# A seven-product first layer for the last two units of an attention and MLP kernel, and a new order for its head and tail

## The chip, the cores and the metric

The kernel runs on one core of one Trainium2 chip. The metric is device time in microseconds (us), the median of several runs. A profiled execution gives the span from the first to the last instruction, and its own time beside it.

## The reference

Inputs are q, k and v, each 4 batches × 8 heads × 768 positions × 64, eight memory positions per head (`mem_k`, `mem_v`), a gain `g_ln` of 512, and the weights `w_ch1` (512 × 2048) and `w_ch2` (2048 × 512), all float32. The two parts, shortened:

```python
for c in range(768 // 32):                         # chunks of 32 queries
    l_start, r_end = max(0, 32*c - 16), min(768, 32*c + 32 + 8)
    k_full = concatenate([mem_k, k[:, :, l_start:r_end]], axis=2)
    v_full = concatenate([mem_v, v[:, :, l_start:r_end]], axis=2)
    a = softmax(q[:, :, 32*c : 32*c + 32] @ k_full.T / sqrt(64))
    out[:, :, 32*c : 32*c + 32] = a @ v_full
x  = out.transpose(0, 2, 1, 3).reshape(4, 768, 512)
xn = (x - mean(x)) / sqrt(var(x) + 1e-6) * g_ln
y  = x + maximum(xn @ w_ch1, 0) @ w_ch2
```

## The kernel before

The 3072 tokens are 24 tiles `t` of 128 tokens, six per batch. Two tiles are a unit `u`, so there are 12 units (`NP = 12`). Operands are float16, sums float32.

Attention for a tile: `qk_products` (scores, L320), `row_max` and `less_max` on VectorE (L329, L332), `weights` (exponential, ScalarE, L342), `pt_products` and `pt_copy` (transpose of the weights, L351, L359), `val_products` (L371, into the two-bank buffer `two`), `tokens` (division by the row sum, VectorE, L380 to L387). Then the norm: `shift` subtracts the mean (GpSimd L394 or ScalarE L398), `square` and `root_of` give the scale, `x_products` transposes the tile (L427) and `x_copy` multiplies by the gain into `xT` (VectorE, L436).

The MLP for a unit of 256 tokens: the first layer is `up_products` (L455): eight groups `s`, each two blocks of 128 hidden columns times four slices of 128 inputs, so eight products of 256 columns. `relu_up` moves a group to `rT` (L447). The second layer is `down7` (L532): the unit's two tiles and the halves of the hidden and the output dimension make a 2 × 2 block product, done with seven block products of eight matmuls in place of eight. For this it needs four sums of `rT` blocks (`r_sum` into `RS`, VectorE, L526) and, once per kernel, four sums of weight blocks (`w2_sum` into `T`, L511). `add_to` adds each product, scaled, to the token tile `xs` (L539), and `store` writes the tile out (L544, SyncE's queue).

PSUM has eight banks: `one` (2), `upb` (2), `dnb` (2) and `two` (2 together). A product waits until the last reader of its bank is done.

The schedule is manual: each engine runs its instructions in the order in which the program names them. Three parts follow one another:

- A head, L603 to L977, written out item by item: loads, transposes, attention of the first ten tiles, units 0 and 1, and the first layer of unit 2. It contains `warm` products (L599): multiplications of zeros that nobody reads, 21 in all. Loads go out on GpSimd's queue; eight can be under way, and a ninth waits for the first.
- A loop over units 3 to 11 with 16 steps each. Even steps do `up` of unit `u` (banks `upb`), odd steps `down7` of unit `u − 1` (banks `dnb`); a table `plan` puts the attention, norm and `r_sum` work of later tiles at given steps.
- A tail: `down7` of unit 11, with its sums.

Of the kernel before, what the change touches and what calls it, by code (L numbers as in the profile page):

```python
# [11 lines left out]
ALU = mybir.AluOpType  # L12
AX = mybir.AxisListType


@with_exitstack
def kernel(
# [416 lines left out]
    def x_copy(t, pv):  # L434
        i = t % 2
        nc.vector.tensor_tensor(  # L436
            out=xT[(t // 2) % 3][:, :, 128 * i : 128 * i + 128],
            in0=pv.rearrange("p (d c) -> p d c", d=4),
            in1=free(g_col, 0, [[1, 4], [0, 128]]), op=ALU.mult,
        )  # L440
# [53 lines left out]

    def w2_block(i, o, n):
        c = w2c[2 * i + n]
        return c[:, :, 256 * o : 256 * o + 256]
# [15 lines left out]
    def r_block(u, i, o):  # L513
        return rT[u % 2][:, 8 * o : 8 * o + 8, 128 * i : 128 * i + 128]

    def r_sum(u, k, lo=0, hi=8):

        if k == 0:
            a, b, op = r_block(u, 1, 0), r_block(u, 1, 1), ALU.add
        elif k == 1:  # L520
            a, b, op = RS[0], r_block(u, 0, 0), ALU.subtract
        elif k == 2:
            a, b, op = r_block(u, 0, 0), r_block(u, 1, 0), ALU.subtract
        else:
            a, b, op = r_block(u, 0, 1), RS[1], ALU.subtract
        nc.vector.tensor_tensor(  # L526
            out=RS[k][:, lo:hi, :], in0=a[:, lo:hi, :], in1=b[:, lo:hi, :], op=op
        )
# [19 lines left out]
    def down7_products(u, part, p):  # L548
# [4 lines left out]
        def total(k):  # L553
            return lambda n: T[k][:, n, :]

        left, right, add = (
            lambda: (r_block(u, 0, 0), block(0, 0), False),
            lambda: (r_block(u, 0, 1), block(1, 0), False),
            lambda: (RS[1], total(1), True),
            lambda: (RS[0], total(0), False),  # L560
            lambda: (RS[2], total(2), True),
            lambda: (RS[3], block(1, 1), True),
# [22 lines left out]
    def ready_v(i, eng):  # L585
        eng.memset(V[i][:, :, :, 64:VW], 1.0)
        eng.memset(V[i][0:16, 0, :, :], 0.0)
        eng.memset(V[i][96:128, NG - 1, :, :], 0.0)
        eng.tensor_copy(
            out=V[i][96:128, NG - 1, :, 64:VW],  # L590
            in_=free(last[96:128, 0:1], 0, [[0, H], [0, VW - 64]]),
        )

# [14 lines left out]
    nc.vector.memset(V[0][:, 0:4, :, 64:VW], 1.0)  # L608
    nc.vector.memset(V[0][0:16, 0, :, 64:VW], 0.0)
# [4 lines left out]
    warm(7, upb[0])  # L614
    load_octets(0, 0, k, 0, 0, 48, (0,))
    load_octets(0, 0, k, 0, 0, 48, (1,))
    load_octets(1, 0, q, 0, 0, 32, (1,))
    copy_on("A")(out=mem16, in_=mem32)
    make_identity(nc, identity)
    mem_products(one[0])  # L620
    mem_copy(one[0], "V")
    mem_cols(KT[0], memT[:, 0:4, :], "V")
    mem_ends(KT[0], memT[:, 0:4, :], "A")
    load_octets(1, 0, q, 0, 0, 32, (0,))
    warm(6, one[1])
    tk0 = turn(raw[0][0], 0, 48, one[1])
    load_octets(2, 0, v, 0, 0, 48, (0,))
    mem_cols(VT, memT[:, 16:20, :], "V")
    load_octets(2, 0, v, 0, 0, 48, (1,))
    to_stream(KT[0], tk0, 0, "V", 48, 0)  # L630
    load_octets(1, 1, q, 0, 32, 64, (0,))
    tk1 = turn(raw[0][0], 1, 48, upb[0])
    to_stream(KT[0], tk1, 1, "V", 48, 0)
    load_octets(1, 1, q, 0, 32, 64, (1,))
    load_octets(0, 1, k, 0, 48, 48, (1,))
    warm(1, upb[1])
    tq1 = turn(raw[1][0], 1, 32, upb[1])
    to_rows(0, tq1, 1, "V", 32, 0, 0, 16)
    mix_into(whole[0], raw[2][0], 0, 96, "V")
    load_octets(2, 1, v, 0, 48, 48, (0,))  # L640
    load_octets(2, 1, v, 0, 48, 48, (1,))
    tq0 = turn(raw[1][0], 0, 32, dnb[0])
    load_octets(0, 1, k, 0, 48, 48, (0,))
    to_rows(0, tq0, 0, "A", 32, 0, 0, 16)
    warm(4, dnb[1])
    s0 = qk_products(0, dnb[1])
    tv0 = turn_whole(whole[0], 0, 96, one[0])
    to_stream(VT, tv0, 0, "V", 48, 0)
    load_w1(0)
    mix_into(whole[0], raw[2][0], 1, 96, "A")  # L650
    to_rows(0, tq0, 0, "A", 32, 0, 16, 32)
    nc.gpsimd.memset(V[0][:, 4:NG, :, 64:VW], 1.0)
    to_rows(0, tq1, 1, "A", 32, 0, 16, 32)
    tv1 = turn_whole(whole[0], 1, 96, one[1])
    to_stream(VT, tv1, 1, "A", 48, 0)
    s1 = qk_products(1, upb[0])
    row_max(1, s1)
    warm(2, dnb[0])
    v2 = v_products(2, dnb[0])
    load_octets(1, 0, q, 1, 0, 48, (0,))  # L660
    load_v_group(1, 11, 1)
    load_w1(3)
    v1 = v_products(1, upb[1])
    load_w1(1)
    mix_into(whole[3], raw[1][1], 1, 128, "A")
    v0 = v_products(0, one[0])
    v_copy(0, v0, "A")
    row_max(0, s0)
    v_copy(1, v1, "A")
    less_max(0, s0)  # L670
    weights(0)
    load_octets(1, 0, q, 1, 0, 48, (1,))
    less_max(1, s1)
    weights(1)
    tQ1 = turn_whole(whole[3], 1, 128, one[1])
    nc.gpsimd.memset(last, 1.0)
    mix_into(whole[3], raw[1][1], 0, 128, "V")
    v3 = v_products(3, one[0])
    v_copy(2, v2, "V")
    p0 = pt_products(0, dnb[1])  # L680
    pt_copy(0, p0, "V")
    mix_into(whole[2], raw[2][1], 1, 96, "V")
    v_copy(3, v3, "A")
    mix_into(whole[2], raw[2][1], 0, 96, "P")
# [4 lines left out]
    p1 = pt_products(1, upb[1])  # L689
    pt_copy(1, p1, "V")  # L690
    val_products(0)
    tokens(0)
    tV1 = turn_whole(whole[2], 1, 96, upb[0])
    load_w2(0)
    to_rows(0, tQ1, 1, "A", 64, 32)
    tQ0 = turn_whole(whole[3], 0, 128, dnb[0])
    mix_into(whole[1], raw[0][1], 0, 96, "A")
    tV0 = turn_whole(whole[2], 0, 96, dnb[1])
    to_stream(VT, tV0, 0, "A", 48, 48)
    load_w1(2)  # L700
# [36 lines left out]
    up_products(0, 1, upb[1])
    relu_up(0, 1, upb[1], "A")
    row_max(2, s2)
    less_max(2, s2)  # L740
    weights(2)
    up_products(0, 0, upb[0])
    up_products(0, 2, one[0])
    relu_up(0, 2, one[0], "A")
    up_products(0, 6, dnb[0])
    p2 = pt_products(2, dnb[1])
    load_v_group(1, 9, 0)
    v_copy(10, v10, "A")
    load_v_group(1, 9, 1)
    root_of(1)  # L750
    pt_copy(2, p2, "V")
    nc.gpsimd.memset(V[0][96:128, NG - 1, :, :], 0.0)
    nc.gpsimd.tensor_copy(
# [3 lines left out]
    load_v_group(1, 6, 1)  # L757
    up_products(0, 7, upb[1])
    relu_up(0, 6, dnb[0], "A")
    relu_up(0, 7, upb[1], "A")  # L760
    val_products(2)
    v9 = v_products(9, one[0])
    relu_up(0, 0, upb[0], "V")
    tokens(2)
    shift(2, "A")
    square(2)
    ready_v(1, nc.gpsimd)
    s3 = qk_products(3, one[1])
    row_max(3, s3)
    less_max(3, s3)  # L770
    up_products(0, 3, dnb[1])
    v_copy(9, v9, "V")
    down_products(0, 0, dnb[0])
    weights(3)
    down_products(1, 0, upb[0])
    relu_up(0, 3, dnb[1], "A")
    x2 = x_products(2, upb[1])
    x_copy(2, x2)
    up_products(0, 5, one[1])
    relu_up(0, 5, one[1], "V")  # L780
    p3 = pt_products(3, one[0])
    root_of(2)
    load_v_group(1, 4, 1)
    pt_copy(3, p3, "V")
    lq01 = turn_whole(mixed[1], 1, 96, dnb[1])
    to_rows(1, lq01, 1, "A", 48, 0)
    up_products(0, 4, upb[1])
    relu_up(0, 4, upb[1], "A")
    load_octets(1, 1, q, 1, 48, 48, (0,))
    val_products(3)  # L790
    tokens(3)
    v8 = v_products(8, one[1])
    s4 = qk_products(4, one[0])
    down_products(1, 1, upb[0])
    row_max(4, s4)
    less_max(4, s4)
    down_products(0, 1, dnb[0])
    v_copy(8, v8, "A")
    lq00 = turn_whole(mixed[1], 0, 96, dnb[1])
    shift(3, "A")  # L800
    nc.gpsimd.memset(memv16[:, :, :, 64:VW], 1.0)
    x3 = x_products(3, upb[1])
    x_copy(3, x3)
    down_products(0, 2, dnb[0])
    w2_sum(0)
    load_v_group(1, 0, 0)
    weights(4)
    square(3)
    load_octets(1, 1, q, 1, 48, 48, (1,))
    p4 = pt_products(4, one[1])  # L810
    load_octets(0, 1, k, 1, 48, 48, (1,))
    pt_copy(4, p4, "A")
# [272 lines left out]
```

## Time and profile before

| | |
|---|---|
| median of 3 runs | 225.61 us (224.96 to 226.55) |
| the profiled execution | 225.04 us, span 223.3 us |
| TensorE busy | 215.1 us, 96% of the span |
| VectorE, ScalarE, GpSimd busy | 164.8 us, 130.3 us, 114.4 us |
| granted TensorE clock | 1.0 in every slice |
| moved by DMA | 23.24 MB, mean 104 GB/s |

A row of a timeline has the start, the duration, the engine, the source line and the operation, then output and inputs, how many were merged, and the idle time before them with what ended it. Durations of successive instructions on an engine overlap by about a tenth of a microsecond, and TensorE's products overlap more, so their cost is read from start to start. A row of a group has busy time, the mean in ns of one, and the idle time before with its releasers.

### The profile page before, as it was taken

The numbers are of one execution on the slowest core, as the hardware profiler recorded it, in microseconds if no ns is written. First come the engines' busy times: TensorE is split into PE (matmuls) and PEld (weight loads), VectorE is DVE, ScalarE is ACT, GpSimd is POOL, SyncE is SP. The second block draws the span as 40 slices with busy tenths as digits, with TensorE's granted clock in tenths as the row PEclk, the third lists the DMA queues.
The fourth block names the chain that finished last, engine by engine and source line by source line (L and its number), as shares of the span: only waits on it lengthen the run. The fifth ranks groups of instructions, "written<-read, shape, count | busy, mean of one in ns | idle before, by whom it ended". The sixth has DMA issues, their size and how long they took to land.

```text
span 223.3 us, 8291 instructions
## 1 busy us (share of the span) xinstructions
PE 215.1 (96%) x3597; PEld 188.9 (85%) x3597; DVE 164.8 (74%) x367; ACT 130.3 (58%) x248; POOL 114.4 (51%) x195
## 2 busy tenths in 40 slices
PE   6987999999999999999999999999999999999994
PEld 2555877689888899999999999999999899999983
DVE  1588667979898886994886996994875876747373
ACT  3198875877785288288357198198266365443320
POOL 7958399989889717957346927321121130320000
PEclk9999999999999999999999999999999999999999
DMA  5999999999999994995934975942002002011022
GB/s 74 191 204 204 211 212 208 134 175 113 126 98 135 164 113 80 121 92 96 185 29 108 132 91 110 91 76 97 3 3 94 3 3 94 3 50 47 0 97 97
DMA packets 43449, 23.24 MB, mean 104 GB/s; under 512 B 30004, under 2 KB 39796, under 8 KB 43364
## 3 DMA queue, kind: packets, MB, share of 16 engines
q0 software_dynamic: 38416, 14.48, 55.3%
q1 hardware_dynamic: 4996, 8.22, 12.8%
q8 instruction: 28, 0.46, 0.8%
q14 instruction: 9, 0.07, 0.1%
HBM read 29.02 MB, written 6.29 MB: 158 GB/s over the span
## 4 chain that ended last, share of the span: by engine, by line
PE 78%; DMA 14%; POOL 3%; DVE 1%; issue 1%; ACT 0%; SPq 0%; POOLq 0%
PE upb L455 30%; PE dnb L532 28%; DMA w1c<-in_moe_w_ch_dram 5%; PE two L371 3%; DMA raw<-in_q_dram 3%; DMA V<-memv 3%; PE one L272 3%; DMA raw<-in_k_dram 2%; PE one L320 2%; PE one L427 2%; POOL raw L105 2%; PE one L351 2%; PE dnb L455 2%; PE upb L481 2%; PE dnb L481 2%; PE one L455 1%
## 5 line engine op out<-in xcount | busy, mean ns | idle before, releaser
L455 PE MATMUL upb<-xT,w1c 128*128 128x256 f16 x656 | 84.7, 273 | 0.3 <-ACT rT L447 0.3
L455 PEld LDWEIGHTS <-w1c 128*128 128x128 f16 x768 | 81.1, 114 | 2.3 <-issue 0.5
L447 ACT ACTIVATE rT<-upb 128x512 f16<-128x512 f32 x81 | 47.1, 597 | 30.9 <-PE upb L455 30.8
L539 DVE SCALAR_TENSOR_TENSOR xs<-dnb,rstd,xs 128x256 f32<-128x256 f32 x75 | 36.1, 481 | 24.1 <-PE dnb L532 23.1
L532 PEld LDWEIGHTS <-RS 128*128 128x128 f16 x352 | 33.6, 98 | 3.6 <-issue 0.2
L342 ACT ACTIVATE P<-sub 128x512 f16<-128x512 f32 x24 | 15.1, 631 | 31.4 <-DVE sub L332 31.3
L532 PE MATMUL dnb<-T,RS 128*128 128x256 f16 x256 | 32.8, 273 | 0.0
L394 POOL TENSOR_SCALAR xn<-xs,nmean 128x512 f16<-128x512 f32 x18 | 12.7, 704 | 31.2 <-PE upb L455 17.5
L532 PEld LDWEIGHTS <-rT 128*128 128x128 f16 x264 | 25.3, 98 | 2.5
L414 POOL TENSOR_SCALAR veps<-ssq 128x1 f32<-128x1 f32 x24 | 4.8, 200 | 40.7 <-ACT sq L407 40.0
L532 PE MATMUL dnb<-w2c,rT 128*128 128x256 f16 x176 | 22.6, 273 | 0.0
L526 DVE TENSOR_TENSOR RS<-rT 128x1024 f16<-128x1024 f16 (+2 forms) x23 | 15.3, 664 | 8.9 <-ACT rT L447 8.9
L407 ACT ACTIVATE sq<-xs,nmean 128x512 f16<-128x512 f32 x24 | 17.3, 722 | 0.1
L381 DVE CUSTOM_DVE_ANT_1 xs<-two,rec 128x512 f32<-128x512 f32 x24 | 16.6, 692 | 0.8
L418 POOL TENSOR_TENSOR rstd<-veps,mhalf 128x1 f32<-128x1 f32 x24 | 14.2, 591 | 2.0
L436 DVE TENSOR_TENSOR xT<-one,g_col 128x512 f16<-128x512 f16 x18 | 12.3, 686 | 3.5 <-PE one L427 3.3
L114 POOL DMA_DIRECT2D V<-in_v_dram x16 | 13.4, 838 | 0.8 <-PE dnb L532 0.7
L359 ACT COPY PT<-one 128x512 f16<-128x512 f16 x18 | 10.5, 585 | 5.4 <-PE one L351 4.6
L239 DVE COPY KT<-one 128x192 f16<-128x192 f16 (+1 forms) x20 | 10.2, 550 | 3.4 <-PE one L226 2.6
L332 DVE TENSOR_TENSOR sub<-one,nmx 128x512 f32<-128x512 f32 x17 | 11.8, 692 | 0.6
L329 DVE TENSOR_REDUCE nmx<-one 128x8 f32<-128x512 f32 x17 | 11.7, 685 | 0.0
L532 PE MATMUL dnb<-T,rT 128*128 128x256 f16 x88 | 11.4, 273 | 0.0
(134 smaller groups left out, 352.1 us busy)
## 6 DMA issues: line engine op xcount, KB each, us to landing
out_dram<-xs SPq DMA_DIRECT2D x23, 256.0 KB, 2.8
raw<-in_k_dram POOLq DMA_DIRECT2D x16, 192.0 KB, 5.8
raw<-in_q_dram POOLq DMA_DIRECT2D x12, 192.0 KB, 6.4
w1c<-in_moe_w_ch_dram POOLq DMA_DIRECT2D x4, 512.0 KB, 11.3
w2c<-in_moe_w_ch_dram POOLq DMA_DIRECT2D x4, 512.0 KB, 13.8
V<-in_v_dram POOLq DMA_DIRECT2D x16, 77.0 KB, 3.7
raw<-in_v_dram POOLq DMA_DIRECT2D x4, 192.0 KB, 7.0
V<-memv SPq DMA_DIRECT2D x6, 120.0 KB
```

The lines of the kernel that those rows point to most:

```text
L114: nc.gpsimd.dma_start(out=V[b % 2][72:128, 0 : NG - 1, h, 0:64], in_=dram(v, base + 16 * D, [[64, 56], [64 * 64, NG - 1], [1, 64]]),)
L342: nc.scalar.activation(out=P[t % 3], in_=sub[t % 2], func=ACTF.Exp, scale=0.125)
L381: nc.vector.tensor_tensor_reduce(out=x.rearrange("p (h d) -> p h d", h=H), in0=free(two, 0, [[128, 8], [1, 64]]), in1=free(r, 0, [[1, 8], ...
L394: nc.gpsimd.tensor_scalar(out=xn[i], in0=x, scalar1=m, scalar2=1.0, op0=ALU.add, op1=ALU.mult,)
L407: nc.scalar.activation(out=sq, in_=xs[t % 9], func=ACTF.Square, bias=nmean[t % 6], scale=1.0, accum_out=ssq[i],)
L418: nc.gpsimd.tensor_tensor(out=rstd[t % 9], in0=veps[i], in1=mhalf, op=ALU.pow)
L436: nc.vector.tensor_tensor(out=xT[(t // 2) % 3][:, :, 128 * i : 128 * i + 128], in0=pv.rearrange("p (d c) -> p d c", d=4), in1=free(g_col, ...
L447: nc.scalar.activation(out=o, in_=i, func=ACTF.Relu)
L455: nc.tensor.matmul(out=p[:, 256 * hb : 256 * hb + 256], lhsT=free(w1c[hc // 4][:, dt, :], hc % 4, [[4, 128]]), rhs=xT[u % 3][:, dt, :], st ...
L526: nc.vector.tensor_tensor(out=RS[k][:, lo:hi, :], in0=a[:, lo:hi, :], in1=b[:, lo:hi, :], op=op)
L532: nc.tensor.matmul(out=p[:, 0:256], lhsT=left[:, n, :], rhs=right(n), start=(n == 0 and not add), stop=(n == 7), skip_group_check=add,)
L539: nc.vector.scalar_tensor_tensor(out=x, in0=p[:, 0:256], scalar=rstd[t % 9], in1=x, op0=ALU.mult, op1=ALU.add,)
```

## The change

Units 10 and 11 become one double unit in their first layer. Input halves (256 of 512 inputs, index `i`), hidden halves (`o`) and the two units (`j`) make a 2 × 2 block product with seven block products in place of eight, in four column groups `c` (two blocks of 128 hidden columns in each half). It needs:

- four sums of first-weight blocks, `w1_sum(k, n, d, engine)`, 16 pieces of 128 × 512, into the old `raw` load buffers (`W1S`); 13 on GpSimd, 3 on VectorE;
- four sums of `xT` blocks, `x_sum(k, engine)`, 128 × 512 each, into the old `P` and `PT` buffers (`XS`); three on GpSimd, one on VectorE;
- per column group two chains of partial totals. A bank is filled by one product and added to by others; in between, `hold` copies its state to SBUF in float32 (ScalarE), and `relu_of_sum` adds a held state to another bank and clips at zero (VectorE, operation `TENSOR_ADD_SAT`). One of the four results of a column group needs no held state (`relu_sum`, ScalarE).

The second layer of units 10 and 11 stays as it was, but reads its hidden blocks from other buffers (`rT_last`, `RS_two`).

The order changes in two places. The loop now ends after unit 7, and all from there on is one list, with units 8 to 11 interleaved; `x_copy` can go to ScalarE there as four pieces, and `r_sum` is often done in halves. The head is replaced by another list with the same products, other banks and engines for some of them, and 18 warm products. In it the constant columns of `V` are set by VectorE at the start, the four blocks of `w_ch1` are loaded in the order 0, 2, 1, 3 right after batch 0's q, k and v, and batch 1's q is loaded behind the weights (before, its first half stood between block 0 and block 3, its second half behind block 1).

The diff, cut:

```diff
+    def x_copy ... engine "A": four nc.scalar.activation(Copy, scale=g_col[:, dt]) of 128 x 128
...
+    def w1_sum(k, n, d, engine):
+        def block(i, o):
+            return w1c[2 * o + n][:, 2 * i + d, :]
+        a, b, op = (
+            (block(0, 1), block(1, 1), ALU.add),
+            (W1S[0][:, n, d, :], block(0, 0), ALU.subtract),
+            (block(0, 0), block(0, 1), ALU.subtract),
+            (block(1, 0), W1S[1][:, n, d, :], ALU.subtract),
+        )[k]
+        on(engine).tensor_tensor(out=W1S[k][:, n, d, :], in0=a, in1=b, op=op)
...
+    def x_sum(k, engine):
+        a, b = (
+            (x_block(0, 1), x_block(0, 0)), (x_block(1, 1), XS[0]),
+            (x_block(1, 1), x_block(0, 1)), (x_block(1, 0), XS[1]),
+        )[k]
+        on(engine).tensor_tensor(out=XS[k], in0=a, in1=b, op=ALU.subtract)
...
+    def up7_products(c, k, p, add):
+        left, right = (
+            (block(0, 0), x_block(0, 0)), (block(1, 0), x_block(1, 0)), (total(3), x_block(1, 1)),
+            (block(1, 1), XS[3]), (total(0), XS[0]), (total(1), XS[1]), (total(2), XS[2]),
+        )[k - 1]
+        for hb in range(2):
+            for d in range(2):
+                nc.tensor.matmul(out=p[:, 256 * hb : 256 * hb + 256], lhsT=left(hb, d),
+                    rhs=right[:, d, :], start=(not add and hb == 0 and d == 0), stop=(d == 1), ...)
...
+    def hold(p, e):
+        nc.scalar.copy(out=e, in_=p)
+    def relu_of_sum(j, o, c, p, e):
+        nc.vector._custom_dve(
+            TENSOR_ADD_SAT, out=r_part(j, o, c), in0=pair(p), in1=pair(e), s0=TOP, s1=0.0)
+    def relu_sum(c, p):
+        nc.scalar.activation(out=r_part(1, 0, c), in_=pair(p), func=ACTF.Relu)
...
-    for u in range(3, NP):
+    for u in range(3, NP - 4):
...
+    r_sum(7, 0)
+    up_products(8, 3, one[1])
+    relu_up(8, 3, one[1], "A")
+    val_products(18)
...
+    x_copy(23, x23, "V")
+    x_sum(0, "V")
+    x_sum(1, "P")
+    x_sum(3, "P")
+    relu_up(9, 0, dnb[1], "A")
+    up_products(9, 1, dnb[1])
+    up_products(9, 4, upb[0])
+    relu_up(9, 4, upb[0], "A")
+    w1_sum(3, 0, 1, "P")
+    relu_up(9, 1, dnb[1], "A")
+    add_to(17, 0, one[0])
+    store(17)
+    up7_products(0, 1, one[1], False)
+    r_sum(8, 3)
+    hold(one[1], held[0][0])
+    up_products(9, 7, one[0])
+    relu_up(9, 7, one[0], "V")
+    up7_products(0, 2, upb[0], False)
+    up7_products(1, 1, dnb[1], False)
+    hold(dnb[1], held[1][0])
+    down7_products(8, 5, dnb[0])
+    add_to(16, 1, dnb[0])
+    up_products(9, 6, one[0])
...
+    up7_products(2, 4, one[0], True)
+    add_to(18, 1, dnb[1])
+    store(18)
+    down7_products(10, 0, upb[0])
+    relu_of_sum(0, 1, 2, one[0], held[0][1])
+    r_sum(11, 0, 4, 8)
+    up7_products(3, 4, one[1], True)
...
+    down7_products(11, 6, dnb[0])
+    store(15)
+    add_to(21, 1, upb[0])
+    down7_products(10, 6, upb[0])
+    r_sum(11, 3, 4, 8)
+    r_sum(11, 3, 0, 4)
+    add_to(23, 0, dnb[0])
+    store(23, 0, 256)
+    add_to(21, 0, upb[0])
+    down7_products(11, 5, one[1])
+    add_to(22, 1, one[1])
+    store(21)
+    store(22)
```

In the new head, around the stretch that the prediction follows:

```diff
+    load_octets(1, 1, q, 0, 32, 64, (0,))
+    load_w1(0)
+    load_w1(2)
+    load_w1(1)
+    weights(0)
+    load_w1(3)
...
+    mix_into(whole[3], raw[1][1], 0, 128, "P")
+    load_w2(1)
+    tQ0 = turn_whole(whole[3], 0, 128, dnb[0])
...
+    load_octets(0, 0, k, 1, 0, 48, (0,))
...
+    shift(0, "P")
+    x0 = x_products(0, upb[0])
...
+    shift(1, "A")
...
+    x1 = x_products(1, upb[1])
+    x_copy(1, x1)
+    v6, v5, v4, v10 = v_products(6 / 5 / 4 / 10)
+    s2 = qk_products(2, one[1])
+    up_products(0, 0, upb[1])
+    up_products(0, 5, one[0])
+    up_products(0, 2, upb[0])
```

More of the change, by code (lines that the diff above doesn't have):

```diff
@@ L636 @@
[L636 to L648, printed above, removed]
@@ L779 @@
[L779 to L795, printed above, removed]
@@ new lines @@
+    val_products(22)
+    x_copy(21, x21, "A")
+    root_of(19)
+    up_products(9, 3, dnb[0])
+    relu_up(9, 3, dnb[0], "A")
+    up_products(9, 0, dnb[1])
+    w1_sum(1, 0, 1, "P")
+    square(20)
+    square(21)
+    w1_sum(0, 1, 0, "V")
+    add_to(14, 1, one[1])
+    store(14)
+    tokens(22)
+    shift(22, "P")
+    p23 = pt_products(23, upb[1])
+    pt_copy(23, p23, "V")
+    down7_products(8, 2, one[0])
+    add_to(16, 0, upb[0])
+    x20 = x_products(20, one[1])
+    x_copy(20, x20, "A")
@@ new lines @@
+    store(16)
+    up7_products(0, 5, one[1], True)
+    x_sum(2, "P")
+    up7_products(1, 7, dnb[0], False)
+    up7_products(0, 7, one[0], False)
+    relu_of_sum(1, 1, 1, dnb[0], held[1][2])
+    up7_products(1, 3, dnb[1], True)
+    hold(one[1], held[0][2])
+    relu_of_sum(1, 1, 0, one[0], held[0][2])
+    w1_sum(2, 1, 1, "P")
+    relu_up(9, 2, upb[1], "A")
+    r_sum(9, 0)
+    r_sum(9, 1)
+    relu_sum(1, dnb[1])
+    root_of(21)
+    up7_products(0, 3, one[1], True)
+    down7_products(9, 0, upb[0])
```

906 lines of the change are left out of this document (585 added, 321 removed).

## The prediction

> **What bounds the kernel now.** I read the page first: busy shares, the clock, and the chain that ended last.
>
> ```profile
> span 223.3 us, 8291 instructions
> PE 215.1 (96%) x3597; PEld 188.9 (85%) x3597; DVE 164.8 (74%) x367; ACT 130.3 (58%) x248; POOL 114.4 (51%) x195
> PE   6987999999999999999999999999999999999994
> PEclk9999999999999999999999999999999999999999
> GB/s 74 191 204 204 211 212 208 134 175 113 126 98 135 164 113 80 121 92 96 185 29 108 132 91 110 91 76 97 3 3 94 3 3 94 3 50 47 0 97 97
> PE 78%; DMA 14%; POOL 3%; DVE 1%; issue 1%; ACT 0%; SPq 0%; POOLq 0%
> ```
>
> TensorE is the bound: full in every slice but the first few and the last, at the full granted clock, and 78% of the chain. So a product taken away is worth its own time if nothing begins to wait. A busy TensorE may still hide small waits, so next come its waits after the front and its stretches (TensorE, weight load, VectorE, ScalarE, GpSimd; then clock, DMA share, GB/s).
>
> ```profile
> PE upb L455 <- ACT rT L447: 0.3, 1, 0.3
> PE one L272 <- DVE sub L332: 0.2, 1, 0.2
> 0.00:24.27 24.27, 19.98 (x414) 12.31 (x414) 15.18 (x39) 15.06 (x29) 19.35 (x36) 1.00 1.08 171
> 155.04:220.10 65.06, 65.02 (x900) 59.88 (x897) 43.70 (x94) 27.97 (x54) 8.85 (x18) 1.00 0.11 40
> ```
>
> From 30 us on TensorE waits 0.5 us in all. In units 8 to 11 and the tail (155 to 220) VectorE is 67% busy, ScalarE 43%, GpSimd 14%: these have room for the additions of a seven-product form. Third, the timeline, for the price of a product and for both ends.
>
> ```profile
> 24.27 1.94 PE L455 MATMUL upb<-xT,w1c 128*128 128x256 f16 x16
> 26.30 1.07 PE one L455 x8
> 14.42 11.83 DMA w1c<-in_moe_w_ch_dram
> ...
> 212.77 1.04 PE L455 MATMUL upb<-xT,w1c 128*128 128x256 f16 x8
> 213.64 1.91 PE L532 MATMUL dnb<-w2c,rT 128*128 128x256 f16 x16
> 219.03 1.04 PE L532 MATMUL dnb<-T,rT 128*128 128x256 f16 x8
> 220.10 0.48 DVE xs L539
> ```
>
> Eight 256-column products start 213.64 − 212.77 = 0.87 us before the next group, so one costs 0.109 us. The first layer begins at 24.27 us, and its third group starts at 26.30, when a block of the first weight has landed (14.42 + 11.83 = 26.25). At the end, 223.3 − 220.58 = 2.7 us pass between the last addition and the end of the span: the last store.
>
> **The change part by part.** *The double unit.* Units 10 and 11 needed 2 × 8 × 8 = 128 first-layer products; the seven-product form needs 4 column groups × 7 × 4 = 112. 16 × 0.109 = **−1.75 us** on the path, sure as long as TensorE stays full. The second layer's count is unchanged.
>
> What it adds lies on other engines. Prices:
>
> ```profile
> L381 DVE CUSTOM_DVE_ANT_1 xs<-two,rec 128x512 f32<-128x512 f32 x24 | 16.6, 692 | 0.8
> L489 DVE SCALAR_TENSOR_TENSOR xs<-dnb,rstd,xs 128x512 f32<-128x512 f32 x1 | 0.8, 752 | 0.0
> L539 DVE SCALAR_TENSOR_TENSOR xs<-dnb,rstd,xs 128x256 f32<-128x256 f32 x75 | 36.1, 481 | 24.1 <-PE dnb L532 23.1
> L526 DVE TENSOR_TENSOR RS<-rT 128x1024 f16<-128x1024 f16 x21 | 14.4, 687 | 8.9 <-ACT rT L447 8.9
> L526 DVE TENSOR_TENSOR RS<-rT 128x256 f16<-128x256 f16 x1 | 0.3, 293 | 0.0
> L436 DVE TENSOR_TENSOR xT<-one,g_col 128x512 f16<-128x512 f16 x18 | 12.3, 686 | 3.5 <-PE one L427 3.3
> L447 ACT ACTIVATE rT<-upb 128x512 f16<-128x512 f32 x81 | 47.1, 597 | 30.9 <-PE upb L455 30.8
> L394 POOL TENSOR_SCALAR xn<-xs,nmean 128x512 f16<-128x512 f32 x18 | 12.7, 704 | 31.2 <-PE upb L455 17.5 <-DVE nmean L387 12.8 <-PE upb L481 0.8
> L259 POOL COPY raw<-raw 96x1024 f16<-96x1024 f16 x6 | 6.0, 1032 | 5.5 <-DMA raw<-in_q_dram 3.4 <-PE one L532 1.8 <-DMA raw<-in_k_dram 0.4
> ```
>
> ScalarE: 16 evictions (12 `hold`, 4 `relu_sum`) in place of the 16 ReLUs, 0.60 each, so nothing; four moved `x_copy`, four pieces each, at under 0.6 a piece. VectorE: 12 `relu_of_sum`, an operation the trace does not have; the two rows that read one bank and one more operand of 512 give 0.69 to 0.75, so 9.0 us at most. Four sums of 512 at 0.4 (between 0.29 for 256 and 0.69 for 1024) are 1.6; two ReLUs and a copy from ScalarE about 1.8; more halved sums about 0.9; four `x_copy` leave (−2.7). That is 43.7 + 10.6 = 54 us of VectorE in a stretch of 63: 86%, still under TensorE. GpSimd: 13 `w1_sum` and 3 `x_sum`, two tensors in, which the trace does not have either: 0.5 (half of the 1024 copy) to 1.4 (two passes of the 512 shift at 0.70). I take 1.0, 16 us in all; GpSimd has 65 − 9 = 56 us free.
>
> Shares don't show single waits, so I went down the new list with start-to-start times (an eviction begins 0.2 us after its last product's slot and takes 0.6 to 0.75). Times count from the start of `up_products(8, 3)`. The tightest places: `up7_products(2, 4)` needs a bank from `relu_of_sum(1, 1, 2)`, free at 49.45, wanted at 49.9. `down7_products(11, 6)` needs `add_to(23, 1)` by 59.9, done 59.6; `down7_products(10, 6)` needs `add_to(21, 1)` by 60.8, done 60.5; `down7_products(11, 5)` needs `r_sum(11, 3)` by 61.6, done 61.2. Everywhere else there is half a microsecond or more. So the list costs nothing by this walk, with 0.3 us as the smallest cover; 0 to +2 us (twenty places that each lose 0.1) is the bound.
>
> `val_products(18)` comes 2.6 us earlier (from 3.6 to 1.0 us after unit 8 starts). It needs batch 3's keys and values, and the GB/s line falls to 3 in slice 28 (150.7 us), before 155.0: landed.
>
> *The front.* Three of the 21 warm products go (fillers, nothing on the path), the batch 1 query load goes behind the weights, and the work is reordered. In the old order 4076 KB, the needed block included, had been queued when that block landed at 26.25; in the new order 3840 KB. The 236 KB less at 204 GB/s are 1.2 us: about 25.1. The third first-layer group then no longer waits for it. What else sets the start: the twelfth input load is queued behind 2304 KB as before, about 17.3 us (26.25 less 1772 KB at 204 GB/s). From there: regrouping on GpSimd 1.05, a weight issue, a mask and a key issue on the same queue to 19.8, `shift(0)` to 20.5, its transpose, `shift(1)` on ScalarE to 21.7, its transpose to 22.1, then five groups without a wait (1.75), and the first layer starts at 23.8 instead of 24.27. One value block (0.35) is still to be done then, and the 0.28 us of waiting (26.30 against 24.27 + 1.75) goes: 0.47 − 0.35 + 0.28 = 0.4, taken as **−0.5 us**, with −2.0 (half of some 4 us of gaps in that walk gone) and +1.5 (loads 1.5 us later) as bounds. The 0.5 us of waits after 30 us stand in stretches that are all reordered; I take **−0.3**, from −0.5 to +1.
>
> *The end.* `store(22)` is a full row, not a half, issued 0.9 us behind `store(21)`.
>
> ```profile
> DMA to landing us min/median/max: 2.0/2.8/4.3
> ```
>
> Median 2.8 against the 2.7 at the end now, and two transfers that overlap: **+0.3**, from 0 to +1.6 (the longest row).
>
> Sum: −1.75 − 0.5 − 0.3 + 0.3 = −2.25 against the profiled execution's 225.04 (span 223.3 and 1.74 around it): 222.8. The runs shown lie from 224.96 to 226.55 with median 225.61, so this execution was at the fast end; 225.61 − 2.25 = 223.4. I say **223.1 us**.
>
> [...]
>
> ```profile
> 11.21 0.41 DVE L259 COPY T<-raw 96x1024 f16<-96x1024 f16 x1
> 16.89 1.15 DVE L259 COPY T<-raw 96x1024 f16<-96x1024 f16 x1
> 16.70 1.05 POOL L259 COPY T<-raw 96x1024 f16<-96x1024 f16 x1
> 191.16 0.68 DVE L526 TENSOR_TENSOR RS<-rT,RS 128x1024 f16<-128x1024 f16 x1
> 191.42 0.98 POOL L394 TENSOR_SCALAR xn<-xs,nmean 128x512 f16<-128x512 f32 x1 [6.79 <-DVE nmean L387]
> ```
>
> The same copy takes VectorE 0.41 us alone and 1.15 when GpSimd began a copy 0.19 us before: it ends 0.29 us after GpSimd's (18.04 against 17.75). GpSimd's shift grows from 0.70 to 0.98 across a sum of two halves on VectorE. [...]
>
> **Rivals.** *VectorE is locked out (slower).* Behind `x_copy(23)` GpSimd has five sums in a row (`x_sum` 1, 3, 2; `w1_sum(3, 0, 1)`, `(2, 1, 1)`) from 28.45; VectorE's `r_sum(8, 3)` is due at 28.8, with `relu_up(9, 7)` and `add_to(16, 1)` behind it, and TensorE wants it for `down7_products(8, 5)` at 31.2. If GpSimd keeps the memory for all five at p each, the stall is 28.45 + 5p + 0.65 − 31.2 = 5p − 2.1: 2.9 us at p = 1.0, which eats the gain, and 4.9 at 1.4, two passes, which I take for this case: **228.0 us**. It is slower than before from p = 0.9 on (5p − 2.1 over 2.4). [...] For it: the rows above. Against it: the copy at 16.89 got in between two GpSimd instructions (the next began at 17.70), and one lost sum alone ends r_sum at 30.1, in time.
>
> *Late evictions (no change).* Twenty handovers lose 0.1 each, +2.0: **225.1 us**. For it: 0.3 us covers, VectorE at 86%. Against: TensorE ran 65 us before with one bank in turn and no wait.
>
> *The front is worth more.* If half the gaps in my walk are not there, −2.0 in place of −0.5: **221.5 us**.
>
> *The clock falls back.* The fillers show it, and a gap of the old front:
>
> ```profile
> 20.45 0.51 PE L272 MATMUL one<-identity,T 96*128 96x96 f16 x8 [0.70 <-POOL T L259]
> L599 PE MATMUL one<-zeros x6: 606/634/634, 5.4 to 7.5; 128*128 128x512 f16 x6
> L599 PE MATMUL dnb<-zeros x6: 379/379/390, 10.5 to 13.2; 128*128 128x512 f16 x6
> ```
>
> 634 ns early, 379 from 10.5 us on, so TensorE speeds up after some 8 us. With three fillers fewer it could fall back; 28 products at half speed, 28 × 0.109 = 3 us, would give **226.1 us**. Against: gaps of 0.75 us at most in my walk, and the old front had 0.7 without a slower row behind them.
>
> **How the numbers follow.** Forecast 0.48, its own range 221.6 to 224.6 (front and store bounds); more from the front 0.14; late evictions 0.15; the clock 0.06; lock-out 0.17. 1%, about what a measurement of this kernel tells from no change, lies at 223.35. Of the forecast 0.33 is under it, with the front's 0.14: faster 0.47. Within: 0.15 + 0.15 + 0.06 = 0.36. Slower: 0.17, the lock-out. The range, 220.9 to 226.6, leaves out most of the lock-out and the far end of the front.
>
> **What would show it.** Right: `up7_products` at 112 products of 0.109, no TensorE wait over 0.3 us after unit 8, `relu_of_sum` at 0.69 to 0.75, first-layer start near 23.8, the last store 2.8 to 3.2 after the last addition. The lock-out would show as an `r_sum` over 1.5 us beside GpSimd sums, with TensorE waiting for a sum or a ReLU near `down7_products(8, 5)`; late evictions as many waits of 0.1 to 0.5 on banks; the clock as 256-column products over 0.109 apart after 24 us. A TensorE start-up later than 25 us makes the front's term wrong, whatever the tail does.

## The result and the profile after

| | before | after |
|---|---|---|
| median | 225.68 us (224.96 to 227.15, 9 runs) | 224.3 us (223.88 to 225.35, 9 runs) |
| ratio | | 0.994, 95% interval 0.9916 to 0.9963 |
| profiled execution | 225.04 us, span 223.3 | 224.56 us, span 222.8 |

The change gains 0.6%, some 1.4 us; the forecast was 223.1 us, and its terms added up to 2.25. Rows of the page after:

```profile
span 222.8 us, 8324 instructions
PE 213.6 (96%) x3578; PEld 188.3 (84%) x3578; DVE 178.3 (80%) x396; ACT 132.0 (59%) x260; POOL 128.2 (58%) x203
PEclk9996999999999999999999999999999999999999
```

TensorE is still the bound, but one slice has its clock at 0.6, which before had nowhere. The timeline (first group of the first layer, third group, first group of unit 3, first group of unit 8, last products and last addition):

```profile
24.88 1.06 PE L464 MATMUL upb<-xT,w1c 128*128 128x256 f16 x8
...
26.65 1.04 PE L464 MATMUL upb<-xT,w1c 128*128 128x256 f16 x8
...
71.69 1.04 PE L464 MATMUL upb<-xT,w1c 128*128 128x256 f16 x8
...
156.05 1.04 PE L464 MATMUL one<-xT,w1c 128*128 128x256 f16 x8
...
218.22 1.04 PE L643 MATMUL one<-w2c,RS 128*128 128x256 f16 x8
...
219.30 0.48 DVE L650 SCALAR_TENSOR_TENSOR xs<-one,rstd,xs 128x256 f32<-128x256 f32 x1 [0.39 <-PE one L643]
```

The same points of before, where the prediction does not show them:

```profile
70.78 1.03 PE L455 MATMUL upb<-xT,w1c 128*128 128x256 f16 x8 [0.30 <-ACT rT L447]
```

So the time came and went like this. From unit 8's first product to the last addition's end, 155.04 to 220.58 was 65.54 us, and 156.05 to 219.78 is 63.73: **−1.8**. From there to the end of the span 2.7 became 3.0: **+0.3**. At unit 3, whose loop has not changed, the new kernel is 71.69 − 70.78 = **0.9 us late** (1.0 at unit 8). The tail and the store did what the prediction says; the head, with the waits behind it forecast at −0.8, lost 0.9. These 0.9 us come in two parts: at the third group of the first layer the new kernel is 26.65 − 26.30 = 0.35 late, and the rest arises between there and unit 3.

The waits of TensorE after 24 us, in the view of waits:

```profile
PE dnb L274 <- issue: 0.7, 1, 0.7
PE one L274 <- DVE sub L334: 0.2, 1, 0.2
```

This view shows none in the tail. The windows of the head (TensorE, weight load, VectorE, ScalarE, GpSimd; then clock, DMA share, GB/s) and TensorE's transposes there:

```profile
18.00:20.00 2.00, 1.35 (x16) 1.21 (x14) 1.70 (x6) 1.72 (x4) 1.96 (x5) 0.73 1.25 210
20.00:22.00 2.00, 2.00 (x49) 1.71 (x48) 0.97 (x3) 1.75 (x2) 1.95 (x3) 0.50 1.23 202
```

```profile
17.71 1.04 POOL L261 COPY T<-raw 128x1024 f16<-128x1024 f16 x1 [2.79 <-DMA raw<-in_q_dram]
18.80 0.98 PE L274 MATMUL dnb<-identity,T 128*128 128x128 f16 x8 [0.65 <-POOL T L261]
19.57 1.06 PE L274 MATMUL one<-identity,T 128*128 128x128 f16 x8
20.57 0.63 PE L373 MATMUL two<-V,PT 64*32 64x65 f16 x32
22.41 0.72 ACT L400 ACTIVATE xn<-xs,nmean 128x512 f16<-128x512 f32 x1 [0.67 <-DVE nmean L389]
23.19 0.40 PE L429 MATMUL upb<-identity,xn 128*128 128x128 f16 x4 [0.44 <-ACT xn L400]
```

By the profile's clock records TensorE's clock is at half from 18.90 to 22.31 us, 3.41 us. In this stretch lie the transposes of the last 64 query columns (18.80, 19.57), tile 1's attention product (20.57) and tile 0's transpose. `shift(1)` on ScalarE ends at 22.41 + 0.72 = 23.13, where the prediction had 21.7, and tile 1's transpose can start only then.

### The profile page after: what moved, and what is told of

It reads as the page before. It is cut to its first block, busy times and chain, and to the rows that moved or that the text cites. A ratio compares the mean times of both kernels' runs of the same rounds, so it can differ in the third digit from the quotient of the medians.

```text
span 222.8 us, 8324 instructions
## 1 busy us (share of the span) xinstructions
PE 213.6 (96%) x3578; PEld 188.3 (84%) x3578; DVE 178.3 (80%) x396; ACT 132.0 (59%) x260; POOL 128.2 (58%) x203
## 4 chain that ended last, share of the span: by engine, by line
PE 85%; DMA 4%; POOL 4%; DVE 3%; issue 1%; ACT 1%; DVEq 0%; POOLq 0%
PE upb L464 22%; PE dnb L643 20%; PE one L464 6%; PE one L643 5%; DMA raw<-in_q_dram 4%; PE upb L643 4%; PE two L373 4%; PE one L274 3%; POOL raw L107 3%; PE dnb L464 2%; PE dnb L578 2%; PE one L578 2%; PE one L429 2%; PE one L322 2%; PE dnb L490 2%; PE upb L490 2%
## 5 line engine op out<-in xcount | busy, mean ns | idle before, releaser
L464 PEld LDWEIGHTS <-w1c 128*128 128x128 f16 x640 | 67.4, 114 | 1.7
L464 PE MATMUL upb<-xT,w1c 128*128 128x256 f16 x448 | 58.3, 273 | 0.0
L456 ACT ACTIVATE rT<-upb 128x512 f16<-128x512 f32 x53 | 30.9, 595 | 17.6 <-PE upb L464 17.6
L650 DVE SCALAR_TENSOR_TENSOR xs<-dnb,rstd,xs 128x256 f32<-128x256 f32 x54 | 25.9, 479 | 11.3 <-PE dnb L643 9.5
L643 PE MATMUL dnb<-T,RS 128*128 128x256 f16 x184 | 23.9, 273 | 0.0
L637 DVE TENSOR_TENSOR RS<-rT 128x1024 f16<-128x1024 f16 x18 | 13.5, 754 | 5.4 <-ACT rT L456 5.4
L464 PE MATMUL one<-xT,w1c 128*128 128x256 f16 x136 | 17.4, 273 | 0.0
L409 ACT ACTIVATE sq<-xs,nmean 128x512 f16<-128x512 f32 x24 | 17.3, 720 | 0.1
L456 ACT ACTIVATE rT<-one 128x512 f16<-128x512 f32 x15 | 9.1, 606 | 5.8 <-PE one L464 5.7
L249 ACT COPY QD<-one 128x768 f16<-128x768 f16 (+2 forms) x12 | 9.4, 784 | 5.0 <-PE one L228 4.1
L274 PEld LDWEIGHTS <-raw 96*128 96x128 f16 x192 | 10.5, 98 | 1.5 <-issue 1.2
```

The source lines that it names most:

```text
L274: nc.tensor.matmul(out=pv[:, rows * r : rows * r + rows], lhsT=m[0:rows, jj, r, :], rhs=identity[0:rows, 0:rows], is_transpose=True, start ...
L409: nc.scalar.activation(out=sq, in_=xs[t % 9], func=ACTF.Square, bias=nmean[t % 6], scale=1.0, accum_out=ssq[i],)
L456: nc.scalar.activation(out=o, in_=i, func=ACTF.Relu)
L464: nc.tensor.matmul(out=p[:, 256 * hb : 256 * hb + 256], lhsT=free(w1c[hc // 4][:, dt, :], hc % 4, [[4, 128]]), rhs=xT[u % 3][:, dt, :], st ...
L643: nc.tensor.matmul(out=p[:, 0:256], lhsT=left[:, n, :], rhs=right(n), start=(n == 0 and not add), stop=(n == 7), skip_group_check=add,)
L650: nc.vector.scalar_tensor_tensor(out=x, in0=p[:, 0:256], scalar=rstd[t % 9], in1=x, op0=ALU.mult, op1=ALU.add,)
```

## The experiments

*The two halves.* `oldhead_newtail` has the head and loop of before up to unit 7 and the list from unit 8 on; `newhead_oldtail` the new head and the loop and tail of before.

```diff
 oldhead_newtail, against the kernel before
-    for u in range(3, NP):
+    for u in range(3, NP - 4):
...
+    r_sum(7, 0)
+    up_products(8, 3, one[1])
...
 newhead_oldtail, against the changed kernel
-    for u in range(3, NP - 4):
+    for u in range(3, NP):
...
-    r_sum(7, 0)
-    up_products(8, 3, one[1])
...
```

> The old head and the loop up to unit 7, then the new list from unit 8 on. Both theories (clock, order of the head) say that the tail alone is worth -1.8 us and its last full-row store costs +0.3, by the profiles: before less 1.5, some 224.2 us, ratio 0.993, last product 1.8 us earlier than before, granted clock 1.0. If the new head loses 1.0 us in every run, as the two profiles say, this must lie 1.0 under the changed kernel of the same chip (223.3 against 224.3); if the profiled execution was an unlucky one, the two are equal.

> The new head, then the old loop and tail. The head costs 0.9 to 1.0 us by the profiles: 226.6 us, ratio 1.004, a stretch of half clock near 19 to 22 us, unit 3 starting near 71.7 us instead of 70.8. If that stretch was a matter of one execution, 225.7, ratio 1.000.

Measured: `oldhead_newtail` 223.78 us, ratio 0.9911 (0.9882 to 0.9941); `newhead_oldtail` 226.5 us, 1.0021 (0.9996 to 1.0046). So the new tail is worth some 2.0 us, more than the whole change (1.5 were expected; the interval, 1.3 to 2.7, holds both), and the new head costs about half a microsecond (its interval reaches from −0.1 to +1.0): the sum is what was measured. Of the two cases in the expectations, a loss of 1.0 in every run or none, neither fits: the truth lies between them.

*Is it the clock, or the fillers?* `fill` puts eight fillers into the gaps of the new head; `old_nofill` takes from before the three fillers that the new head lacks.

```diff
 fill: new kernel with
+    warm(3, two[:, 0:512])
     p0 = pt_products(0, dnb[1])
...
     p1 = pt_products(1, one[1])
+    warm(2, two[:, 0:512])
...
     tV1 = turn_whole(whole[2], 1, 96, upb[1])
+    warm(3, dnb[0])
```

> The changed kernel with eight more filler products (3 before p0, 2 between p1 and val_products(0), 3 after tV1), all in gaps in which TensorE waited 0.7, 0.6 and 0.65 us. Clock theory: too little TensorE work between 15 and 19 us let the clock fall; with the fillers it stays at full speed, the first layer starts at 24.0 instead of 24.9, 0.9 us less than the changed kernel: 223.4, ratio 0.990. Order theory: the clock may stay up, but the start is set by the loads and ScalarE's queue: first layer still at 24.7 to 24.9, 224.3 us, ratio 0.994.

> The kernel before without the three fillers that the new head leaves out (two before v_products(2), one before x_products(0)). If these three held the clock: a stretch of half clock appears and it is 0.3 to 1.0 us slower, ratio 1.002 to 1.004. If the gaps of the new order let it fall: clock 1.0, 225.7 us, ratio 1.000.

Measured: `fill` 224.66 us, 0.9932 (0.9903 to 0.9962); `old_nofill` 225.76 us, 0.9998 (0.9975 to 1.0022), its mean clock at 0.998 or more in 10 of 12 runs. So in the old order the three fillers neither held the clock nor cost anything. In `fill`'s profile the slow stretch lies earlier, from 14.41 us, ahead of the eight fillers, and the transposes run at full speed:

```profile
14.00:18.00 4.00, 4.00 (x48) 2.82 (x45) 2.68 (x7) 3.31 (x6) 0.60 (x2) 0.57 1.24 204
18.00:20.00 2.00, 2.00 (x50) 1.10 (x49) 1.64 (x7) 1.31 (x3) 1.34 (x2) 1.00 1.23 207
```

```profile
18.66 1.04 POOL L261 COPY T<-raw 128x1024 f16<-128x1024 f16 x1 [2.23 <-DMA raw<-in_q_dram]
19.75 0.62 PE L274 MATMUL dnb<-identity,T 128*128 128x128 f16 x8
20.21 0.61 PE L274 MATMUL one<-identity,T 128*128 128x128 f16 x8
24.94 1.06 PE L464 MATMUL upb<-xT,w1c 128*128 128x256 f16 x8
```

Two groups of eight are 0.46 us apart here, 0.77 and 1.0 in the changed kernel. But the twelfth load is taken up at 18.66 in place of 17.71, and the first layer starts no earlier. The seven other runs of `fill` granted a mean clock of 0.997 or more, and the median did not fall: the clock theory's 223.4 is not met. The clock alone does not explain the head.

*Tile 1 first.* In the new head tile 1's attention stands behind the two transposes that wait for the twelfth load. It is put ahead of them; besides, `x_copy(1)` goes ahead of `to_stream` of `tK1`, `v4` ahead of `v5`, `up_products(0, 0)` ahead of `v10` and `s2`, and `up_products(0, 4)` ahead of `(0, 2)`.

```diff
 val1_first: new kernel with
     val_products(0)
+    pt_copy(1, p1, "V")
     tokens(0)
...
+    val_products(1)
+    tokens(1)
     tQ0 = turn_whole(whole[3], 0, 128, dnb[0])
...
+    tK0 = turn_whole(whole[1], 0, 96, one[1])
     to_rows(0, tQ0, 0, "A", 64, 32)
-    pt_copy(1, p1, "V")
-    val_products(1)
+    shift(1, "A")
...
-    tokens(1)
     shift(0, "P")
     x0 = x_products(0, upb[0])
...
```

> The changed kernel with one stretch of its head reordered: pt_copy(1), val_products(1), tokens(1) and shift(1) go ahead of the transposes tQ0 and tQ1 of batch 0's last queries, tK0 goes ahead of x0, and up_products(0, 0) ahead of v10 and s2. Order theory (the first layer starts late in the new head because tile 1's chain stands behind two transposes that wait for the twelfth load): x1 moves from 23.2 to about 21.8 us, up_products(0, 0) from 24.9 to 23.0-23.3, and with v10 and s2 then still to do (0.6) the time falls by 0.6 to 1.2 us, to 223.1-223.7 us. Clock theory (the slow stretch of TensorE costs it): the start moves as said where the clock is full, but the time falls by less than 0.3 us. Loads theory (the weight blocks' landings set the pace up to 29 us): TensorE waits for a block instead, the time falls by less than 0.3 us.

Measured: 224.69 us, 0.9949 (0.9929 to 0.997): no gain, against my order theory. The first layer does start earlier, at 24.08 (23.0 to 23.3 were expected), though the twelfth load came at 18.4 there. But `v10` and `s2`, 0.7 us, now stand behind its first group, and the third group starts at 26.66, as in the changed kernel (26.65): the lead is spent there already. A wait follows further on:

```profile
24.08 1.06 PE L464 MATMUL upb<-xT,w1c 128*128 128x256 f16 x8
26.66 1.04 PE L464 MATMUL dnb<-xT,w1c 128*128 128x256 f16 x8
57.99 0.74 POOL L140 DMA_DIRECT2D V<-in_v_dram  x1
58.81 0.18 POOL L416 TENSOR_SCALAR veps<-ssq 128x1 f32<-128x1 f32 x1
59.07 0.56 POOL L420 TENSOR_TENSOR rstd<-veps,mhalf 128x1 f32<-128x1 f32 x1
59.67 0.49 DVE L650 SCALAR_TENSOR_TENSOR xs<-dnb,rstd,xs 128x256 f32<-128x256 f32 x1 [1.89 <-POOL rstd L420]
60.19 0.48 DVE L650 SCALAR_TENSOR_TENSOR xs<-upb,rstd,xs 128x256 f32<-128x256 f32 x1
60.73 0.41 PE L322 MATMUL upb<-KT,QD 64*32 64x64 f16 x32 [1.03 <-DVE xs L650]
```

Read from the bottom: TensorE waits 1.03 us for a bank, which waits for `add_to(2, 0)` on VectorE, which waits for `root_of(2)` on GpSimd, which stands in that queue behind value loads. `fill` and `nosums` (below) have 0.7 us of the same wait. Unit 3 starts at 71.93 us, 0.2 after that of the changed kernel.

*That queue.* `root_early` and `root_val1` move two `root_of` forward, the one in the changed kernel, the other in `val1_first`.

```diff
     root_of(1)
+    root_of(2)
     load_v_group(1, 3, 0)
...
     shift(4, "P")
+    root_of(3)
...
     load_v_group(1, 6, 0)
-    root_of(2)
...
     r_sum(1, 0)
-    root_of(3)
```

> The changed kernel with root_of(2) and root_of(3) moved on GpSimd's queue from behind the batch 1 value loads and mix(1, 1) to 45-48 us, behind root_of(1) and shift(4). In four of six profiles of the new head TensorE waits 0.7 to 1.0 us at 60 us for add_to(2, 0), which waits for root_of(2) in that queue. Queue theory (the new head's lead ends there, whatever the start of the first layer is): no wait for add_to(2, 0) is left at 60 us, unit 3 starts at 71.0-71.3 us instead of 71.4-71.9, and the time falls by 0.3 to 0.7 us, to 223.6-224.0. Loads theory (the queue is itself held by the landings of its loads, and the next thing behind it waits as long): another wait on a load or on a later item of GpSimd takes its place, unit 3 starts as before, and the time stays within 0.2 us.

> The same two root_of moved earlier, in the kernel whose head has tile 1's chain first (val1_first: 224.69 us, first layer at 24.08, 1.03 us of waiting for add_to(2, 0) at 60 us, unit 3 at 71.92). Queue theory: that wait goes, unit 3 starts at 70.7-71.0 us, and the time falls by 0.7 to 1.0 us, to 223.7-224.0; so the earlier start, worth nothing alone, is worth something once GpSimd's queue does not end it. Loads theory: as in the kernel beside it, less than 0.3 us.

Measured: `root_early` 224.66 us, 0.9957 (0.9927 to 0.9987); `root_val1` 224.57 us, 0.995 (0.9924 to 0.9977). Neither profile has the wait for `add_to(2, 0)`. For `root_early` that shows little: the changed kernel's own profile had no such wait either, and three of the six earlier profiles of the new head show it (`fill`, `nosums`, `val1_first`), not four, as the expectation has it. The times stay, as the loads theory has it and not as I expected; the new wait that this theory asks for shows in `root_val1` alone, where TensorE waits for GpSimd's copy of a later load and unit 3 starts at 71.78 us. Its third group, at 26.77, had no lead that the moved `root_of` could have kept. `root_early`'s profiled execution met 10.2 us of half clock (unit 3 at 73.13), `root_val1`'s 3.4. The clock of the first and the waits of the second:

```profile
PEclk9995599999999999999999999999999999999998
```

```profile
PE one L274 <- POOL raw L261: 0.4, 1, 0.4
```

*Three repairs at once.* `root_val1_split` halves the last store too (below), and `root_val1_split_fill` adds `fill`'s eight fillers.

> The kernel beside it with the last store in two halves (columns 0 to 255 of tile 22 sent out behind store(20)). With the whole store the end from the last addition was 3.06-3.10 us, with the halves 2.74, so 0.3 us less than the kernel beside it, 223.4-223.7 us by the queue theory; by the loads theory 224.2.

> root_val1_split (224.1 us) with the eight fillers of the kernel fill: three before p0, two behind p1, three behind tV1. In the runs so far with one of the new heads without them, TensorE had a half-speed window of 3.4 us in the head in 65 of 91 (mean granted clock under 0.995), with the old head in 17 of 102, with the eight fillers in 1 of 8; over all runs a window goes with some 0.4 us. Clock theory (these windows are what is left of the new head's loss): at most 3 of 12 runs have a window, and the time falls by 0.3 us, to 223.7-223.9. Loads theory (the landings set the pace, and fillers or clock change little): the windows go, and the time stays at 224.0-224.4. If the fillers themselves delay tile 1's chain, it rises to 224.5 or more.

Measured: 224.1 us, 0.9928 (0.9903 to 0.9954), and 223.74 us, 0.9927 (0.9898 to 0.9955). The first is nearer to the loads theory's 224.2. In microseconds the second is what the clock theory said; but the kernel before was faster by as much in its runs (225.31 against 225.67), and the ratios are the same. The runs do not tell the fillers' gain from none. The profile does show what the head is without the slow stretch:

```profile
PEclk9999999999999999999999999999999999999999
```

```profile
22.07 0.39 PE L429 MATMUL upb<-identity,xn 128*128 128x128 f16 x4
23.31 1.03 PE L464 MATMUL upb<-xT,w1c 128*128 128x256 f16 x8
25.86 1.04 PE L464 MATMUL dnb<-xT,w1c 128*128 128x256 f16 x8
```

Tile 1's transpose is at 22.07, the third group at 25.86, 0.8 us before that of the changed kernel. Unit 3 starts at 71.15 us, still 0.4 after that of before (70.78).

The clocks of all runs, together: a mean granted clock under 0.995 (the 3.41 us at half clock in the changed kernel's profile take its mean to 0.992) had 65 of 91 runs of kernels with a new head without the eight fillers, 19 of 116 with the old head, and 2 of 14 with the eight fillers. Fitted over all runs with a level for each kernel, 0.008 less of the mean clock goes with some 0.4 us (0.2 to 0.7). By this estimate, a share of such runs that is 0.55 higher (65 of 91 against 19 of 116) at 0.4 us each, the clock is some 0.2 us of the head's loss.

*The tail's terms.* `plus16` puts back sixteen products; `nosums` lets GpSimd fill its sixteen sums with zeros, so the products that use them work on zeros.

```diff
 plus16: up7_products with
+        for extra in range(4 if k == 1 else 0):
+            nc.tensor.matmul(out=p[:, 0:256], lhsT=left(0, 0), rhs=right[:, 0, :], start=True, stop=True)
 nosums: w1_sum (and x_sum alike) with
+        if engine == "P":
+            nc.gpsimd.memset(W1S[k][:, n, d, :], 0.0)
+            return
```

> The changed kernel with four products of 256 columns more in each of the four up7_products(c, 1), sixteen in all, whose result the next product overwrites: the count of the eight-product form in the seven-product order. If each product on the path costs 0.109 us, the time rises by 1.75 us, to 226.0 us, and no new wait shows. If the tail has hidden waits that a longer TensorE stretch fills (late evictions), it rises by less than 1.3 us.

> The changed kernel with each of GpSimd's sixteen sums (w1_sum, x_sum) replaced by a fill of the same 128x512 output with zeros, which reads nothing; so the first layer of the last two units works on zeros where these sums stood, and its time alone is read. Covered theory (a lost sum of VectorE's stays off the path): r_sum(8, 3) falls from 1.48 to about 0.69 us, the nine r_sum of 1024 from 816 to about 690 ns in the mean, and the time stays within 0.2 us of the changed kernel (224.1-224.5 us). Lock-out theory (the sums cost something on the path after all): the time falls by 0.5 us or more, to 223.8 or less.

Measured: `plus16` 226.13 us, 1.0022 (1.0001 to 1.0042), 1.8 us over the changed kernel, as expected, and no wait in its tail. Its stretch from 156.06 to 221.39 is 1.6 us longer than the changed kernel's, 0.100 a product:

```profile
156.06 1.04 PE L464 MATMUL one<-xT,w1c 128*128 128x256 f16 x8
220.91 0.48 DVE L654 SCALAR_TENSOR_TENSOR xs<-one,rstd,xs 128x256 f32<-128x256 f32 x1 [0.39 <-PE one L647]
```

`nosums`: 224.52 us, 0.9941 (0.9911 to 0.9971), as the changed kernel; in its profile the stretch from unit 8 to the last addition is 63.60 us, 0.1 less than 63.73. Beside the sums `r_sum(8, 3)` takes 1.48 us on VectorE, and 0.68 without them. First the changed kernel around `r_sum(8, 3)`, then `nosums`:

```profile
184.65 1.16 POOL L554 TENSOR_TENSOR P<-xT,P 128x512 f16<-128x512 f16 x1 [1.36 <-DVE P L554]
184.88 1.48 DVE L637 TENSOR_TENSOR RS<-rT,RS 128x1024 f16<-128x1024 f16 x1
185.89 1.49 POOL L554 TENSOR_TENSOR PT<-xT,P 128x512 f16<-128x512 f16 x1
186.41 0.69 DVE L458 TENSOR_SCALAR rT<-one 128x512 f16<-128x512 f32 x1
```

```profile
184.72 0.68 DVE L641 TENSOR_TENSOR RS<-rT,RS 128x1024 f16<-128x1024 f16 x1
```

and their groups, in the same order:

```profile
L637 DVE TENSOR_TENSOR RS<-rT,RS 128x1024 f16<-128x1024 f16 x9 | 7.3, 816 | 0.0
```

```profile
L641 DVE TENSOR_TENSOR RS<-rT,RS 128x1024 f16<-128x1024 f16 x9 | 6.5, 728 | 0.0
```

`r_sum(8, 3)` begins 0.23 us behind the start of a GpSimd sum of 1.16 us and ends at 186.36, 0.55 us behind that sum's end; the next GpSimd sum, begun at 185.89, takes 1.49 us and ends at 187.38, and the one behind it 1.16 again. TensorE shows no wait there.

*The last store.* `oldhead_split` is `oldhead_newtail` with tile 22 stored in halves.

```diff
     store(20)
+    store(22, 0, 256)
...
-    store(22)
+    store(22, 256, 512)
```

> The kernel before up to unit 7 (its head, its loop) with the new tail, and the last store of a full row as two halves: columns 0 to 255 of tile 22 go out behind store(20), only 256 to 511 at the end. If the full row at the end costs the 0.3 us by which the end grew (2.72 to 3.02 us from the last addition), the end is 2.7-2.8 us and the time 0.2-0.3 us under the same kernel with the whole store (223.78), so 223.5 us. If the end is the fixed time of a transfer whatever its size, it stays at 3.0 and 223.8 us.

Measured: 224.0 us, 0.9927 (0.9899 to 0.9955). In the profile the end falls as expected, from 222.05 − 218.95 = 3.1 to 222.49 − 219.76 = 2.7 us; the 0.4 cannot be seen in the medians, where the time did not fall.

```profile
218.46 0.48 DVE L650 SCALAR_TENSOR_TENSOR xs<-one,rstd,xs 128x256 f32<-128x256 f32 x1 [0.39 <-PE one L643]
```

```profile
219.28 0.48 DVE L650 SCALAR_TENSOR_TENSOR xs<-one,rstd,xs 128x256 f32<-128x256 f32 x1 [0.39 <-PE one L643]
```

## Why the prediction was right where it was, and wrong where it was

The forecast was 223.1 us and 224.3 was measured, inside the range of 220.9 to 226.6. The two terms of the head came out with the wrong sign; the number still fits because the range was wide and the tail's gain larger than the head's loss.

- *The double unit, −1.75.* Right: −1.8 in the stretch, and the sixteen products put back cost 1.6 there and 1.8 in the median.
- *The list runs without a wait.* Right: the view of waits shows none after unit 8, with VectorE at 54.89 of 67 us:

```profile
155.00:222.00 67.00, 64.26 (x896) 59.32 (x894) 54.89 (x117) 31.26 (x69) 27.23 (x33) 1.00 0.12 45
L596 DVE CUSTOM_DVE_ANT_0 rT<-one,QD 128x512 f16<-128x512 f32 x3 | 2.1, 684 | 0.0
L542 POOL TENSOR_TENSOR raw<-w1c,w1c 128x512 f16<-128x512 f16 x4 | 4.7, 1181 | 0.0
```

  `relu_of_sum` took 0.68 to 0.69 where 0.69 to 0.75 was said. GpSimd's sum took 1.15 to 1.16 in most cases and up to 1.59, where 1.0 was taken with a bound of 1.4. One reading behind this term was off by a slice: the GB/s line falls to 3 from 156.3 us on, not from 150.7. Batch 3's loads were in time all the same, since in the profile of before no DMA ran from 151 to 153 us.
- *The lock-out.* `r_sum(8, 3)` was not held until five sums were done: it took 1.48 us beside GpSimd's sums and 0.68 in `nosums`, so 0.80 more, less than one sum of 1.16, and the GpSimd sum behind took 1.49. The case against it, that a lost sum ends `r_sum` in time, held: `nosums` shows a price on the path of 0.1 us in the profile and none in the median.
- *The last store, +0.3.* Right (2.7 to 3.0), and in the profile halving it takes it away.
- *The front, −0.5.* This failed: 0.35 late at the third group, in place of 0.5 early. The walk went down GpSimd's queue to `shift(0)`; the path that ended last was another, tile 1's attention on TensorE, which stands behind the two groups of transposes that wait for the twelfth load. This load was taken up 0.4 us later than reckoned (17.71, not 17.3), and the two groups, 0.46 us each at full clock (`fill`), took 0.77 and 1.0 at half: together 1.2 of the 1.4 us by which `shift(1)` was late. The five groups behind it took 0.4 less than reckoned (23.52 to 24.88), so the first layer began 1.1 late, at 24.88 in place of 23.8. The third group did not wait for its weight block, as said, but this landed at 25.85 and not at 25.1, so that a start at 23.8 would have met it. By the prediction's own sign, a start later than 25 us, the term would have passed.
- *The waits after 30 us, −0.3.* This failed too: they grew from 0.5 to 0.9 us. I took them to shrink, without a walk through that stretch. In the changed kernel's profile it is the wait of 0.7 us at 52.4, whose cause was not found; `newhead_oldtail` has it too. In three other profiles of the new head a wait of 0.7 to 1.0 us stands at 60 us, since the new order has `root_of(2)` behind value loads on GpSimd; `plus16` has neither. Moving `root_of` brought nothing in the medians, so this wait is not shown to be what the head lost.
- *The clock as a rival.* I looked for it after 24 us, behind missing fillers. It came at 18.9, and in most runs of the new head. In `old_nofill`, the old order without the three fillers that were left out, 2 of 12 runs have a mean clock under 0.995; in the new order eight more leave 2 of 14, in place of 65 of 91. So the clock fell more often with the new order than with the old one (19 of 116), and rarely once its gaps were filled. Its size was less than the 3 us of the rival, whose 28 products at half speed stand on no row of before: some 0.4 us for each 0.008 of the mean clock.
- What stays open: at a full clock, too, the new head is no faster than the old one (the median of its five runs at 0.997 or more in `newhead_oldtail` is 226.5, of 77 such runs of before 225.7). With order, queue, clock and store mended its ratio is 0.9927; that of the old head with the new tail, which is the simpler kernel of the two, is 0.9911. I have not separated how much of the loss is the order, the queue, and the landing times, each under half a microsecond. One pair of profiles cannot tell them apart. In `oldhead_split`, whose head and loop are those of before, unit 3 starts 1.0 us later than in the profile of before; its clock first goes up at 14.06 us, not at 9.71:

```profile
71.77 1.03 PE L464 MATMUL upb<-xT,w1c 128*128 128x256 f16 x8 [0.30 <-ACT rT L456]
```

## What to carry to other kernels

A product less on a bound TensorE was worth its full time here (0.100 us each in `plus16`, 0.109 reckoned), and GpSimd's sixteen sums cost 0.1 us in the profile (63.73 against 63.60 without them): the slowed `r_sum` was still in time. A start that comes earlier is not yet a lead: `val1_first` started its first layer 0.8 us earlier and had nothing left of it at the third group, since other work had moved behind the first. So compare a later point, and walk through every queue up to the steady loop; look on a queue with loads for small items that stand behind them (`root_of(2)` on GpSimd's, and 1.03 us of TensorE's waiting in `val1_first`). Where a change has two places, run each alone: here the one was worth 0.9%, and the other took about a quarter of it back, with an interval that just reaches nothing.

## What was not expected of the hardware

- TensorE's clock fell to half at 18.90 us with no long gap of TensorE ahead of it: in the 3.41 us before it was busy for 1.76 us, and from 14 us on its longest gap was the 0.68 us ahead of `p0`. In `root_early`, whose clock went up at 4.13 and fell at 17.78, the last two stretches of the same length before the fall have 2.32 and 1.56 us, and only the second was followed by a fall. The changed kernel's gap and stretch, then the two of `root_early`:

```profile
15.78 0.40 PE L353 MATMUL dnb<-identity,P 128*128 128x128 f16 x4 [0.68 <-ACT P L344]
...
15.49:18.90 3.41, 1.76 (x50) 1.22 (x51) 2.53 (x10) 2.84 (x6) 1.19 (x2) 1.00 1.24 206
...
10.96:14.37 3.41, 2.32 (x74) 1.91 (x76) 2.53 (x8) 2.67 (x7) 2.03 (x3) 1.00 1.24 204
14.37:17.78 3.41, 1.56 (x30) 0.94 (x24) 2.10 (x6) 2.92 (x5) 0.55 (x1) 1.00 1.24 205
```

  In the clock records the slow stretch of the changed kernel's head is 3.41 us long and begins 10.24 us after the clock went up (8.66 to 18.90); that of `root_early` is 10.2 us long and begins 13.65 us after (4.13 to 17.78). In the profile of before TensorE was busy for 2.07 us from 15.49 to 18.90, and the clock stayed at 1.0. What makes the clock fall is not shown here.
- TensorE waited 0.7 us at 52.4 inside a group of eight transposes, with nothing named as the releaser; 0.8 in `newhead_oldtail`, 0.3 in `root_val1_split`, and not at all in the others. Its cause was not found.
